# Holding the last two pairs' loads behind two divisions, and issuing the second k before the first weight quarter

## The chip, the cores and the metric

The kernel runs on one core of a Trainium2 chip. The metric is the device time of one execution in microseconds (us); the time given is the median over runs. Profiles come from one execution taken by the hardware profiler. TensorE (PE in the profile) multiplies matrices, VectorE (DVE) and ScalarE (ACT) work on tiles, GpSimd (POOL) issues the loads, SyncE (SP) issues the moves inside the chip and the stores.

## The reference

Two stages. First an attention in chunks: q, k and v have shape (8, 8, 576, 64) (batch, heads, positions, width), the 576 positions fall into 9 chunks of 64, and each chunk attends only to itself:

```python
scores = scale * np.matmul(q_c, k_c.transpose(0, 1, 2, 4, 3))
scores = scores - np.max(scores, axis=-1, keepdims=True)
attn = np.exp(scores)
attn = attn / (np.sum(attn, axis=-1, keepdims=True) + 1e-09)
out = np.matmul(attn, v_c)
```

The result, laid out as x of 4608 tokens by 512, goes through a feed-forward layer that multiplies two branches:

```python
a = x @ w1
b = x @ w2
h = a * b @ w3
return (h @ w_out).astype(np.float32)
```

w1 and w2 are 512 by 1024, w3 is 1024 by 1024, w_out is 1024 by 512. Inputs and output are float32.

## The kernel before

The 4608 tokens are cut into 18 *pairs* p of 256 tokens (four chunks of 64), numbered 0 to 17; two pairs make a *group* of 512 tokens. w3 @ w_out is worked out once on the chip (steps V, W, Z), so that the second half is (a * b) @ w3o.

The order of all work is written out by hand in the string `ORDER`. The kernel runs through it and calls one function for each step; each engine takes its instructions in that order (`tc.keep_in_program_order`), and an engine that waits holds back everything behind it. A step is a letter and its numbers:

- R, K: q and k of pair 0, loaded as float32 by SP and ACT and cast by ScalarE. q, k, v (lines of `load_qk`, `load_v`): loads of pair p, issued on POOL, with a cast to bfloat16 on the way. i0 to i3: a quarter of w1 and of w2, two loads each; o and h: w_out and w3. All of these go through POOL's one queue.
- T p.s (L188): VectorE transposes q (s = 0) or k (s = 1) of pair p. S: scores on TensorE. E (L221): exponential on ScalarE. P: weights times v, on TensorE. N p.u (L248, L251): reciprocal and division of half u of pair p, on VectorE, into `xn`. X (L263, L271): transpose of that half for the second stage.
- From pair 8 on, G (moves of the transposed q and k) and H (moves of the transposed x) are issued on SP, eight DMAs for each G or H of a group: four in G g.0 and four in G g.1.
- A p.j, B p.j: matmuls with w1 and w2; C (L317): ScalarE copies A's result out of PSUM; M (L332): VectorE multiplies it with B's. From pair 4 on one A, B, C, M serves a whole group of two pairs, so that they stand at even p only.
- O: matmuls with w3o; Y (L362): ScalarE copies the result; Q: SP stores it.
- D: dummy matmuls on a tile of zeros, into a PSUM buffer that the next step overwrites. D0 stands ahead of S1, D1 ahead of A0.0.

All results on TensorE go into one PSUM pool of four buffers of two banks. qk tiles have five buffers, `xn` three, v six fixed tiles (`vbuf[p % 6]`). All loads and matmuls go through the helpers `load` (L95) and `mm` (L92), so in the profile all matmuls have the line L92 and all of POOL's loads the line L95.

A load on POOL carries the semaphore that the eighth load before it counts up, and waits for it: eight loads are in flight at most.

Of the kernel before, what the change touches and what calls it, by code (L numbers as in the profile page):

```python
# [7 lines left out]

ORDER = """
R0 R1 v0 q1 i0 k1 v1 i1 i2 q2 k2 v2 i3 q3 k3 v3 q4 k4 v4 o h0 h1 D0.0.16.64 K0 T0.0 K1 T0.1 q5 k5 v5  # L10
S0 T1.0 E0 P0 D0.1.4.512 T1.1 q6 k6 v6 N0.0 S1 D1.0.5.512 X0.0 N0.1 X0.1 A0.0 E1 B0.0 C0.0 P1 M0.0
A0.1 N1.0 X1.0 B0.1 C0.1 N1.1 A0.2 X1.1 B0.2 C0.2 M0.1 A1.0 T2.0 B1.0 C1.0 M0.2 A1.1 T2.1 q7 k7 v7
B1.1 C1.1 M1.0 S2 M1.1 A0.3 E2 T3.0 B0.3 C0.3 P2 M0.3 A1.2 N2.0 X2.0 B1.2 C1.2 N2.1 A1.3 X2.1 B1.3
C1.3 M1.2 A2.0 T3.1 q8 k8 v8 B2.0 C2.0 M1.3 S3 T4.0 A2.1 E3 M2.0 B2.1 T4.1 q9 k9 C2.1 P3 v9 M2.1
A2.2 N3.0 B2.2 C2.2 X3.0 A2.3 N3.1 B2.3 X3.1 C2.3 M2.2 S4 M2.3 A3.0 E4 B3.0 C3.0 A3.1 M3.0 B3.1 C3.1
V0 A3.2 M3.1 B3.2 C3.2 V1 A3.3 M3.2 B3.3 C3.3 V2 W0 M3.3 V3 W1 Z0 V4 V5 W2 Z1 V6 V7 T5.0 Z2 W3 T5.1
q10 k10 T6.0 T6.1 P4 v10 q11 k11 Z3 S5 N4.0 O0 E5 X4.0 N4.1 X4.1 T7.0 O1 T7.1 Y0 Q0 T8.0 P5 v11 q12
k12 Y1 S6 T8.1 O2 Q1 E6 N5.0 X5.0 N5.1 X5.1 O3 T9.0 T9.1 Y2 G4.0 P6 v12 q13 k13 A4.0 N6.0 B4.0 G4.1
Y3 X6.0 N6.1 C4.0 A4.1 X6.1 B4.1 C4.1 M4.0 Q2 S7 Q3 M4.1 A4.2 E7 T10.0 B4.2 C4.2 T10.1 P7 v13 q14
k14 A4.3 M4.2 B4.3 N7.0 C4.3 A4.4 X7.0 M4.3 B4.4 C4.4 N7.1 A4.5 M4.4 B4.5 C4.5 X7.1 S8 M4.5 S9 E8  # L20
A4.6 T11.0 B4.6 E9 T11.1 P8 v14 q15 k15 C4.6 A4.7 M4.6 G5.0 B4.7 C4.7 N8.0 A6.0 M4.7 B6.0 N8.1 C6.0
G5.1 A6.1 X8.0 B6.1 M6.0 C6.1 X8.1 P9 v15 q16 k16 A6.2 M6.1 N9.0 B6.2 C6.2 N9.1 A6.3 M6.2 B6.3 C6.3
X9.0 A6.4 M6.3 B6.4 C6.4 X9.1 A6.5 T12.0 H4.0 B6.5 C6.5 M6.4 A6.6 M6.5 B6.6 T12.1 H4.1 C6.6 S10 S11
M6.6 E10 A6.7 T13.0 B6.7 E11 P10 v16 q17 k17 T13.1 C6.7 O4 M6.7 G6.0 N10.0 N10.1 X10.0 G6.1 P11 v17
Y4 X10.1 O5 N11.0 N11.1 Q4 X11.0 X11.1 T14.0 A8.0 H5.0 Y5 B8.0 T14.1 C8.0 A8.1 M8.0 B8.1 H5.1 C8.1
T15.0 A8.2 B8.2 M8.1 C8.2 T15.1 Q5 A8.3 B8.3 C8.3 M8.2 G7.0 S12 M8.3 S13 E12 A8.4 T16.0 B8.4 E13
G7.1 P12 T16.1 C8.4 A8.5 B8.5 M8.4 C8.5 N12.0 A8.6 M8.5 B8.6 C8.6 N12.1 A8.7 M8.6 B8.7 C8.7 X12.0
P13 M8.7 A10.0 X12.1 B10.0 C10.0 N13.0 A10.1 M10.0 B10.1 N13.1 C10.1 A10.2 X13.0 B10.2 M10.1 C10.2
X13.1 S14 S15 M10.2 E14 A10.3 H6.0 T17.0 B10.3 E15 P14 T17.1 C10.3 A10.4 H6.1 M10.3 B10.4 C10.4
N14.0 A10.5 M10.4 B10.5 G8.0 C10.5 N14.1 A10.6 M10.5 B10.6 C10.6 X14.0 P15 G8.1 X14.1 A10.7 M10.6  # L30
B10.7 N15.0 C10.7 O6 N15.1 M10.7 X15.0 X15.1 H7.0 S16 Y6 S17 O7 E16 E17 H7.1 P16 Y7 O8 Q6 N16.0 Q7
N16.1 X16.0 X16.1 P17 Y8 A12.0 N17.0 Q8 B12.0 N17.1 C12.0 A12.1 X17.0 B12.1 M12.0 C12.1 X17.1 A12.2
M12.1 H8.0 B12.2 C12.2 A12.3 M12.2 B12.3 C12.3 H8.1 A12.4 M12.3 B12.4 C12.4 A12.5 M12.4 B12.5 C12.5
A12.6 M12.5 B12.6 C12.6 A12.7 M12.6 B12.7 C12.7 O9 M12.7 O10 Y9 Q9 A14.0 Y10 B14.0 C14.0 Q10 A14.1
M14.0 B14.1 C14.1 A14.2 M14.1 B14.2 C14.2 A14.3 M14.2 B14.3 C14.3 A14.4 M14.3 B14.4 C14.4 A14.5
M14.4 B14.5 C14.5 A14.6 M14.5 B14.6 C14.6 A14.7 M14.6 B14.7 C14.7 O11 M14.7 O12 Y11 Q11 A16.0 Y12
B16.0 C16.0 Q12 A16.1 M16.0 B16.1 C16.1 A16.2 M16.1 B16.2 C16.2 A16.3 M16.2 B16.3 C16.3 A16.4 M16.3
B16.4 C16.4 A16.5 M16.4 B16.5 C16.5 A16.6 M16.5 B16.6 C16.6 A16.7 M16.6 B16.7 C16.7 O13 M16.7 O14
Y13 Q13 O15 Y14 Q14 O16 Y15 Q15 Y16 Q16 O17
"""  # L40


# [1 line left out]
def kernel(  # L44
# [11 lines left out]
    nc = tc.nc  # L56
    B, H, S, D = q.shape
# [18 lines left out]
    bf = mybir.dt.bfloat16  # L76
# [3 lines left out]
    consts = ctx.enter_context(tc.tile_pool(name="consts", bufs=1))  # L80
# [6 lines left out]
    def inorder(ins):  # L87
        tc.keep_in_program_order(ins)
        return ins

    def mm(*a, **kw):
        return inorder(nc.tensor.matmul(*a, **kw))  # L92

    def load(dst, src):
        return inorder(nc.gpsimd.dma_start(dst, src))  # L95

    def psum(name):
        return ps.tile([P, 2, 512], f32, tag="p", name=name)
# [7 lines left out]
    w3o = wpool.tile([P, FO, DM], bf, name="w3o")  # L106

    zero = consts.tile([P, 512], bf, name="zero")
    inorder(nc.vector.memset(zero[:], 0.0))
    vbuf = [consts.tile([P, 2, H, VW], bf, name=f"vbuf{i}") for i in range(6)]  # L110
    for t in vbuf:
# [2 lines left out]
    def spans(c0, n):  # L114

        at = 0
        while at < n:
            b, c = divmod(c0 + at, NCH)
            m = min(n - at, NCH - c)
            yield at, b, c, m  # L120
            at += m
# [19 lines left out]
    def heads(h):  # L141
        return slice(0, H) if h is None else slice(h * HH, (h + 1) * HH)

    def load_qk(p, which, h=None):
        if p not in qk_t:
            qk_t[p] = io.tile([P, 2, H, 2 * D], bf, tag="qk", bufs=5, name="qk")
        for s in which:
            for at, b, c, m in spans(4 * p, 4):
                load(qk_t[p][at * BL:(at + m) * BL, s, heads(h)],
                     (q, k)[s][b, heads(h), c * CH:(c + m) * CH, :].rearrange("h (p t) d -> p h (t d)", t=2))  # L150

    def load_v(p):
        for u in range(2):
            for at, b, c, m in spans(4 * p + 2 * u, 2):
                load(vbuf[p % 6][at * CH:(at + m) * CH, u, :, 0:D],
                     v[b, :, c * CH:(c + m) * CH, :].rearrange("h p d -> p h d"))
# [17 lines left out]
    qkT_t, qkm_t, s_t, e_t, pv_t, xn_t, xm_t, xt_t = {}, {}, {}, {}, {}, {}, {}, {}  # L174
# [106 lines left out]

    ab_t, ps_t, a_t, o_t = {}, {}, {}, {}

    def do_D(which, p, n, cols):

        d, key = (s_t, p) if which == 0 else (ps_t, (p, 0))
        if key not in d:
            d[key] = psum("z_ps")
        for _ in range(n):
            mm(d[key][:, 0, 0:cols], lhsT=zero[:, 0:P], rhs=zero[:, 0:cols], start=True, stop=True)  # L290
# [97 lines left out]
    def load_q(p, h=None):  # L388
        load_qk(p, (0,), h)

    def load_k(p, h=None):
        load_qk(p, (1,), h)
# [6 lines left out]
    def load_half3(i):  # L399
# [6 lines left out]

    do = {"q": load_q, "k": load_k, "v": load_v, "i": load_w12, "o": load_wo, "h": load_half3, "T": do_T, "S": do_S, "R": do_R, "K": do_K, "E": do_E, "G": do_G, "H": do_H,
          "P": do_P, "N": do_N, "X": do_X, "A": do_A, "B": do_B, "C": do_C, "M": do_M, "D": do_D, "V": do_V,  # L410
          "W": do_W, "Z": do_Z, "O": do_O, "Y": do_Y, "Q": do_Q}
    for step in ORDER.split():
# [31 lines left out]
```

The softmax here doesn't subtract the row's maximum and nothing guards it: scores larger than these inputs give would overflow.

## Time and profile before

| What | us |
|---|---|
| median of 5 runs | 245.42 (244.5 to 246.91) |
| the profiled execution | 245.42 |
| its span, first to last instruction | 243.3 |
| TensorE matmuls busy | 226.2 (93%) |
| VectorE busy | 153.8 (63%) |
| ScalarE busy | 85.1 (35%) |
| POOL busy (issuing loads) | 82.7 (34%) |

The span was run at a granted TensorE clock of 1.0. The median time from issue to landing of a load of 256 KB was 7.8 us for q, 10.6 us for k and 9.9 us for a weight piece; of SP's moves 6.4 us (qkm, 128 KB) and 3.3 us (xt, 64 KB); of a store of 512 KB 4.1 us. In a timeline a line reads: start, duration, engine, line, operation, output<-input, count; in brackets the idle time of the engine before it and what ended that.

### The profile page before, as it was taken

What the parts mean: (1) busy time and instruction counts of PE and PEld (TensorE: products, weight loads), DVE (VectorE), ACT (ScalarE), POOL (GpSimd) and SP (SyncE); (2) the same over time, 40 slices, a digit from 0 to 9 for tenths busy, and PEclk for the clock granted to TensorE, in tenths of its full rate; (3) what the DMA queues carried; (4) which work ended last, traced back from release to release, by engine and by line L of the source; (5) the groups of instructions that cost most, each with busy time, mean ns of one, the idle gap of its engine ahead of it and who ended that gap; (6) DMA issues with size and microseconds to landing.
All of it is one profiled execution on the core that took longest, in us unless ns stands there. A gap on an engine that the chain in (4) does not pass through costs nothing.

```text
span 243.3 us, 6344 instructions
## 1 busy us (share of the span) xinstructions
PE 226.2 (93%) x2731; PEld 120.5 (50%) x2753; DVE 153.8 (63%) x232; ACT 85.1 (35%) x116; POOL 82.7 (34%) x110
## 2 busy tenths in 40 slices
PE   1279989999999989999999999999999999999994
PEld 1238878874445444445444444444444444444443
DVE  1675899699799588999998899918440332143000
ACT  2411423423333344425336334162332432332322
POOL 8847876555985345763750000000000000000000
PEclk9999999999999999999999999999999999999999
DMA  7999999999999999999999923735502200400244
GB/s 178 181 183 180 185 168 201 196 194 169 162 173 218 224 225 260 176 220 194 205 217 255 287 62 80 172 86 202 149 0 89 86 0 0 172 3 1 86 172 172
DMA packets 93595, 37.63 MB, mean 155 GB/s; under 512 B 75008, under 2 KB 86528, under 8 KB 93568
## 3 DMA queue, kind: packets, MB, share of 16 engines
q0 software_dynamic: 82592, 18.88, 83.4%
q1 hardware_dynamic: 9936, 17.83, 24.2%
q10 hardware_dynamic: 1040, 0.52, 0.8%
q8 instruction: 21, 0.34, 0.6%
q14 instruction: 6, 0.05, 0.1%
HBM read 38.80 MB, written 9.44 MB: 198 GB/s over the span
## 4 chain that ended last, share of the span: by engine, by line
PE 77%; DMA 14%; DVE 2%; POOL 2%; issue 2%; ACT 1%; SPq 0%; ACTq 0%; DVEq 0%; POOLq 0%
PE ab_ps L92 43%; PE o_ps L92 24%; DMA w<-in_moe_w_dram 7%; PE w_ps L92 6%; DMA qk<-in_q_dram 3%; PE s_ps L92 3%; PE pv L92 2%; DMA qkm<-qkT 2%; DMA out_dram<-o_sb 2%; POOL vbuf L95 1%; ACT o_sb L362 1%; POOL w L95 1%; DVE xt L263 1%; DVE xn L251 1%; DVE qkT L188 1%
## 5 line engine op out<-in xcount | busy, mean ns | idle before, releaser
L92 PE MATMUL ab_ps<-xt,w 128*128 128x512 bf16 (+1 forms) x681 | 127.0, 342 | 1.7 <-DVE xt L263 1.1
L92 PEld LDWEIGHTS <-w 128*128 128x128 bf16 x704 | 67.2, 98 | 55.8 <-DVE xt L263 1.7
L332 DVE TENSOR_TENSOR ab<-a_sb,ab_ps 128x512 bf16<-128x512 f32 x71 | 47.8, 674 | 44.2 <-ACT a_sb L317 44.2
L317 ACT COPY a_sb<-ab_ps 128x512 f32<-128x512 f32 x71 | 41.6, 586 | 81.2 <-PE ab_ps L92 79.3
L92 PE MATMUL o_ps<-w3o,ab 128*128 128x512 bf16 (+1 forms) x285 | 63.3, 373 | 0.6
L188 DVE STREAM_TRANSPOSE qkT<-qk 128x1024 bf16<-128x1024 bf16 x36 | 45.0, 1289 | 9.6 <-ACT qk L139 5.5
L92 PEld LDWEIGHTS <-ab 128*128 128x128 bf16 x296 | 28.5, 98 | 32.3
L95 POOL DMA_DIRECT2D vbuf<-in_v_dram x40 | 33.9, 855 | 20.5 <-PE pv L92 4.3
L362 ACT COPY o_sb<-o_ps 128x1024 f32<-128x1024 f32 x17 | 17.2, 1012 | 45.5 <-PE o_ps L92 41.3
L251 DVE TENSOR_TENSOR xn<-pv,rc 128x512 bf16<-128x512 f32 x36 | 24.9, 692 | 1.2
L95 POOL DMA_DIRECT2D qk<-in_q_dram x23 | 18.1, 791 | 8.5 <-DMA vbuf<-in_v_dram 2.6
L95 POOL DMA_DIRECT2D qk<-in_k_dram x23 | 18.0, 787 | 7.1 <-DMA vbuf<-in_v_dram 4.3
L221 ACT ACTIVATE e<-s_ps 128x1024 bf16<-128x1024 f32 x16 | 15.9, 1027 | 1.9 <-PE s_ps L92 1.6
L92 PE MATMUL w_ps<-wo,w3T 128*128 128x512 bf16 x62 | 13.9, 379 | 0.1
L271 DVE STREAM_TRANSPOSE xm<-xn 128x512 bf16<-128x512 bf16 x20 | 13.6, 697 | 0.2
L248 DVE RECIPROCAL rc<-pv 128x8 f32<-128x8 f32 x36 | 6.9, 192 | 10.4 <-PE pv L92 10.4
L95 POOL DMA_DIRECT2D w<-in_moe_w_dram x16 | 11.1, 694 | 5.2 <-DMA wo<-in_moe_w_out_dram 2.9
L92 PEld LDWEIGHTS <-e 64*32 64x32 bf16 (+1 forms) x832 | 7.9, 97 | 7.9 <-issue 6.1
L263 DVE STREAM_TRANSPOSE xt<-xn 128x512 bf16<-128x512 bf16 x16 | 11.4, 712 | 0.5
L92 PE MATMUL pv<-vbuf,e 64*32 64x65 bf16 (+1 forms) x832 | 10.1, 198 | 1.1 <-ACT e L221 1.1
L92 PEld LDWEIGHTS <-qkT 32*64 32x64 bf16 x512 | 5.5, 117 | 11.0 <-DVE qkT L188 9.5
L355 DVE COPY o_sb<-o_ps 128x256 f32<-128x256 f32 x1 | 0.4, 426 | 16.0 <-PE o_ps L92 16.0
(23 smaller groups left out, 53.2 us busy)
## 6 DMA issues: line engine op xcount, KB each, us to landing
out_dram<-o_sb SPq DMA_DIRECT2D x17, 512.0 KB, 4.1
qkm<-qkT SPq DMA_DIRECT2D x40, 128.0 KB, 6.4
vbuf<-in_v_dram POOLq DMA_DIRECT2D x32, 128.0 KB, 8.7
w<-in_moe_w_dram POOLq DMA_DIRECT2D x16, 256.0 KB, 9.9
qk<-in_q_dram POOLq DMA_DIRECT2D x11, 256.0 KB, 7.8
qk<-in_k_dram POOLq DMA_DIRECT2D x11, 256.0 KB, 10.6
xt<-xm SPq DMA_DIRECT2D x40, 64.0 KB, 3.3
wo<-in_moe_w_out_dram POOLq DMA_DIRECT2D x4, 256.0 KB, 7.2
```

What stands on the lines that cost most here:

```text
L92: return inorder(nc.tensor.matmul(*a, **kw))
L95: return inorder(nc.gpsimd.dma_start(dst, src))
L188: inorder(nc.vector.transpose(qkT_t[g][:, :, p % 2, s, heads(h)].rearrange("p e h (y t) -> p h t e y", t=2), qk_t[p][:, s, heads(h)].rearr ...
L221: inorder(nc.scalar.activation(e_t[p][:, :, heads(hh)], s_t[p][:].rearrange("p u (h q) -> p u h q", q=CH)[:, :, heads(hh)], Exp, scale=sca ...
L248: inorder(nc.vector.reciprocal(rc[:], pv[:, :, :, D:W]))
L251: inorder(nc.vector.tensor_mul(xn_t[p][:, u], pv[:, :, :, 0:D], rc.to_broadcast([P, 2, 4, D])))
L263: inorder(nc.vector.transpose(new_xt(g)[:].rearrange("p (o t) -> p o t", o=KO)[:, :, t0:t0 + UT] .rearrange("p o (m y) -> p m o y", y=BL), ...
L271: inorder(nc.vector.transpose(xm_t[g][:, u, :, m].rearrange("p o (c y) -> p c o y", y=BL), xn_t[p][:].rearrange("p u r m d -> p (u r) m d" ...
L317: inorder(nc.scalar.copy(a_t[p, j][:], ps_t[p, j][:, 0, :]))
L332: inorder(nc.vector.tensor_mul(o, view(a_t.pop((p, j))[:]), view(ps_t.pop((p, j))[:, 1, :])))
L355: inorder(copy(o_sb[:, u, n0:n1], t[:, 0, 0:n1 - n0]))
L362: inorder(nc.scalar.copy(o_sb[:], ps_t.pop(p)[:]))
```

## The change

Two edits in `ORDER` and one new step, x. In the first line `i0 k1` becomes `k1 i0`: the load of k of pair 1 is issued ahead of the two loads of the first weight quarter. Further down, the loads of pair 16 (q, k from behind v15, v from behind P10) stand together behind N11.1 and a step x11; those of pair 17 stand together behind N12.1 and a step x12. A step x p copies one element of half 1 of `xn` of pair p into a tile of one element, on POOL, so that POOL waits until VectorE has divided that half; the loads that follow on POOL come after. POOL's order of loads is otherwise as it was: x11 comes directly behind v15, then q, k, v of pair 16, then x12, then q, k, v of pair 17, which end POOL's list.

The function w is added too, but no step calls it; D takes one more number, which names the same two tiles as before. On the other engines the instructions and their order stay as they are.

```diff
-R0 R1 v0 q1 i0 k1 v1 i1 i2 q2 k2 v2 i3 q3 k3 v3 q4 k4 v4 o h0 h1 D0.0.16.64 K0 T0.0 K1 T0.1 q5 k5 v5
+R0 R1 v0 q1 k1 i0 v1 i1 i2 q2 k2 v2 i3 q3 k3 v3 q4 k4 v4 o h0 h1 D0.0.0.16.64 K0 T0.0 K1 T0.1 q5 k5
...
-C6.0 G5.1 A6.1 X8.0 B6.1 M6.0 C6.1 X8.1 P9 v15 q16 k16 A6.2 M6.1 N9.0 B6.2
+C6.0 G5.1 A6.1 X8.0 B6.1 M6.0 C6.1 X8.1 P9 v15 A6.2 M6.1 N9.0 B6.2
...
-M6.6 E10 A6.7 T13.0 B6.7 E11 P10 v16 q17 k17 T13.1 C6.7 O4 M6.7 G6.0 N10.0 N10.1 X10.0 G6.1 P11 v17
-Y4 X10.1 O5 N11.0 N11.1 Q4 X11.0 X11.1
+M6.6 E10 A6.7 T13.0 B6.7 E11 P10 T13.1 C6.7 O4 M6.7 G6.0 N10.0 N10.1 X10.0 G6.1 P11 Y4 X10.1 O5
+N11.0 N11.1 x11 q16 k16 v16 Q4 X11.0 X11.1
...
-N12.1 A8.7 M8.6
+N12.1 x12 q17 k17 v17 A8.7 M8.6
...
+    tick = consts.tile([1, 1], bf, name="tick")
...
+    def do_x(p):
+
+        inorder(nc.gpsimd.tensor_copy(tick[:], xn_t[p][0:1, 1, 0, 0, 0:1]))
```

More of the change, by code (lines that the diff above doesn't have):

```diff
@@ L9 @@
 ORDER = """
-R0 R1 v0 q1 i0 k1 v1 i1 i2 q2 k2 v2 i3 q3 k3 v3 q4 k4 v4 o h0 h1 D0.0.16.64 K0 T0.0 K1 T0.1 q5 k5 v5
[L11 to L19, printed above, removed]
@@ L20 @@
-k14 A4.3 M4.2 B4.3 N7.0 C4.3 A4.4 X7.0 M4.3 B4.4 C4.4 N7.1 A4.5 M4.4 B4.5 C4.5 X7.1 S8 M4.5 S9 E8
-A4.6 T11.0 B4.6 E9 T11.1 P8 v14 q15 k15 C4.6 A4.7 M4.6 G5.0 B4.7 C4.7 N8.0 A6.0 M4.7 B6.0 N8.1 C6.0
-G5.1 A6.1 X8.0 B6.1 M6.0 C6.1 X8.1 P9 v15 q16 k16 A6.2 M6.1 N9.0 B6.2 C6.2 N9.1 A6.3 M6.2 B6.3 C6.3
-X9.0 A6.4 M6.3 B6.4 C6.4 X9.1 A6.5 T12.0 H4.0 B6.5 C6.5 M6.4 A6.6 M6.5 B6.6 T12.1 H4.1 C6.6 S10 S11
-M6.6 E10 A6.7 T13.0 B6.7 E11 P10 v16 q17 k17 T13.1 C6.7 O4 M6.7 G6.0 N10.0 N10.1 X10.0 G6.1 P11 v17
@@ L25 @@
[L25 to L36, printed above, removed]
@@ L37 @@
-B16.0 C16.0 Q12 A16.1 M16.0 B16.1 C16.1 A16.2 M16.1 B16.2 C16.2 A16.3 M16.2 B16.3 C16.3 A16.4 M16.3
-B16.4 C16.4 A16.5 M16.4 B16.5 C16.5 A16.6 M16.5 B16.6 C16.6 A16.7 M16.6 B16.7 C16.7 O13 M16.7 O14
-Y13 Q13 O15 Y14 Q14 O16 Y15 Q15 Y16 Q16 O17
+R0 R1 v0 q1 k1 i0 v1 i1 i2 q2 k2 v2 i3 q3 k3 v3 q4 k4 v4 o h0 h1 D0.0.0.16.64 K0 T0.0 K1 T0.1 q5 k5
+v5 S0 T1.0 E0 P0 D0.1.0.4.512 T1.1 q6 k6 v6 N0.0 S1 D1.0.0.5.512 X0.0 N0.1 X0.1 A0.0 E1 B0.0 C0.0 P1
+M0.0 A0.1 N1.0 X1.0 B0.1 C0.1 N1.1 A0.2 X1.1 B0.2 C0.2 M0.1 A1.0 T2.0 B1.0 C1.0 M0.2 A1.1 T2.1 q7 k7
@@ new lines @@
+v7 B1.1 C1.1 M1.0 S2 M1.1 A0.3 E2 T3.0 B0.3 C0.3 P2 M0.3 A1.2 N2.0 X2.0 B1.2 C1.2 N2.1 A1.3 X2.1
+B1.3 C1.3 M1.2 A2.0 T3.1 q8 k8 v8 B2.0 C2.0 M1.3 S3 T4.0 A2.1 E3 M2.0 B2.1 T4.1 q9 k9 C2.1 P3 v9
+M2.1 A2.2 N3.0 B2.2 C2.2 X3.0 A2.3 N3.1 B2.3 X3.1 C2.3 M2.2 S4 M2.3 A3.0 E4 B3.0 C3.0 A3.1 M3.0 B3.1
+C3.1 V0 A3.2 M3.1 B3.2 C3.2 V1 A3.3 M3.2 B3.3 C3.3 V2 W0 M3.3 V3 W1 Z0 V4 V5 W2 Z1 V6 V7 T5.0 Z2 W3
+T5.1 q10 k10 T6.0 T6.1 P4 v10 q11 k11 Z3 S5 N4.0 O0 E5 X4.0 N4.1 X4.1 T7.0 O1 T7.1 Y0 Q0 T8.0 P5 v11
@@ new lines @@
+q12 k12 Y1 S6 T8.1 O2 Q1 E6 N5.0 X5.0 N5.1 X5.1 O3 T9.0 T9.1 Y2 G4.0 P6 v12 q13 k13 A4.0 N6.0 B4.0
+G4.1 Y3 X6.0 N6.1 C4.0 A4.1 X6.1 B4.1 C4.1 M4.0 Q2 S7 Q3 M4.1 A4.2 E7 T10.0 B4.2 C4.2 T10.1 P7 v13
+q14 k14 A4.3 M4.2 B4.3 N7.0 C4.3 A4.4 X7.0 M4.3 B4.4 C4.4 N7.1 A4.5 M4.4 B4.5 C4.5 X7.1 S8 M4.5 S9
+E8 A4.6 T11.0 B4.6 E9 T11.1 P8 v14 q15 k15 C4.6 A4.7 M4.6 G5.0 B4.7 C4.7 N8.0 A6.0 M4.7 B6.0 N8.1
+C6.0 G5.1 A6.1 X8.0 B6.1 M6.0 C6.1 X8.1 P9 v15 A6.2 M6.1 N9.0 B6.2 C6.2 N9.1 A6.3 M6.2 B6.3 C6.3
+X9.0 A6.4 M6.3 B6.4 C6.4 X9.1 A6.5 T12.0 H4.0 B6.5 C6.5 M6.4 A6.6 M6.5 B6.6 T12.1 H4.1 C6.6 S10 S11
@@ new lines @@
+M6.6 E10 A6.7 T13.0 B6.7 E11 P10 T13.1 C6.7 O4 M6.7 G6.0 N10.0 N10.1 X10.0 G6.1 P11 Y4 X10.1 O5
+N11.0 N11.1 x11 q16 k16 v16 Q4 X11.0 X11.1 T14.0 A8.0 H5.0 Y5 B8.0 T14.1 C8.0 A8.1 M8.0 B8.1 H5.1
+C8.1 T15.0 A8.2 B8.2 M8.1 C8.2 T15.1 Q5 A8.3 B8.3 C8.3 M8.2 G7.0 S12 M8.3 S13 E12 A8.4 T16.0 B8.4
+E13 G7.1 P12 T16.1 C8.4 A8.5 B8.5 M8.4 C8.5 N12.0 A8.6 M8.5 B8.6 C8.6 N12.1 x12 q17 k17 v17 A8.7
+M8.6 B8.7 C8.7 X12.0 P13 M8.7 A10.0 X12.1 B10.0 C10.0 N13.0 A10.1 M10.0 B10.1 N13.1 C10.1 A10.2
+X13.0 B10.2 M10.1 C10.2 X13.1 S14 S15 M10.2 E14 A10.3 H6.0 T17.0 B10.3 E15 P14 T17.1 C10.3 A10.4
@@ new lines @@
+H6.1 M10.3 B10.4 C10.4 N14.0 A10.5 M10.4 B10.5 G8.0 C10.5 N14.1 A10.6 M10.5 B10.6 C10.6 X14.0 P15
+G8.1 X14.1 A10.7 M10.6 B10.7 N15.0 C10.7 O6 N15.1 M10.7 X15.0 X15.1 H7.0 S16 Y6 S17 O7 E16 E17 H7.1
+P16 Y7 O8 Q6 N16.0 Q7 N16.1 X16.0 X16.1 P17 Y8 A12.0 N17.0 Q8 B12.0 N17.1 C12.0 A12.1 X17.0 B12.1
+M12.0 C12.1 X17.1 A12.2 M12.1 H8.0 B12.2 C12.2 A12.3 M12.2 B12.3 C12.3 H8.1 A12.4 M12.3 B12.4 C12.4
+A12.5 M12.4 B12.5 C12.5 A12.6 M12.5 B12.6 C12.6 A12.7 M12.6 B12.7 C12.7 O9 M12.7 O10 Y9 Q9 A14.0 Y10
@@ L40 @@
+B14.0 C14.0 Q10 A14.1 M14.0 B14.1 C14.1 A14.2 M14.1 B14.2 C14.2 A14.3 M14.2 B14.3 C14.3 A14.4 M14.3
+B14.4 C14.4 A14.5 M14.4 B14.5 C14.5 A14.6 M14.5 B14.6 C14.6 A14.7 M14.6 B14.7 C14.7 O11 M14.7 O12
+Y11 Q11 A16.0 Y12 B16.0 C16.0 Q12 A16.1 M16.0 B16.1 C16.1 A16.2 M16.1 B16.2 C16.2 A16.3 M16.2 B16.3
+C16.3 A16.4 M16.3 B16.4 C16.4 A16.5 M16.4 B16.5 C16.5 A16.6 M16.5 B16.6 C16.6 A16.7 M16.6 B16.7
+C16.7 O13 M16.7 O14 Y13 Q13 O15 Y14 Q14 O16 Y15 Q15 Y16 Q16 O17
 """
@@ L150, in load_qk, with do_w @@
                      (q, k)[s][b, heads(h), c * CH:(c + m) * CH, :].rearrange("h (p t) d -> p h (t d)", t=2))
+    def do_w(p):
+        inorder(nc.gpsimd.tensor_copy(tick[:], qkT_t[p // 2][0:1, 0, p % 2, 1, 0, 0:1]))
+    def do_x(p):
+        inorder(nc.gpsimd.tensor_copy(tick[:], xn_t[p][0:1, 1, 0, 0, 0:1]))
     def load_v(p):
@@ L282, with do_D @@
     ab_t, ps_t, a_t, o_t = {}, {}, {}, {}
-    def do_D(which, p, n, cols):
-        d, key = (s_t, p) if which == 0 else (ps_t, (p, 0))
+    def do_D(which, p, j, n, cols):
+        d, key = ((s_t, p), (ps_t, (p, j)), (pv_t, (p, 0)))[which]
         if key not in d:
@@ L401, in load_half3 @@
         load_w3(i * n, (i + 1) * n)
-    do = {"q": load_q, "k": load_k, "v": load_v, "i": load_w12, "o": load_wo, "h": load_half3, "T": do_T, "S": do_S, "R": do_R, "K": do_K, "E": do_E, "G": do_G, "H": do_H,
+    do = {"q": load_q, "k": load_k, "v": load_v, "i": load_w12, "o": load_wo, "h": load_half3, "T": do_T, "S": do_S, "R": do_R, "K": do_K, "E": do_E, "w": do_w, "x": do_x, "G": do_G, "H": do_H,
           "P": do_P, "N": do_N, "X": do_X, "A": do_A, "B": do_B, "C": do_C, "M": do_M, "D": do_D, "V": do_V,
```

## The prediction

> **What bounds the kernel now.** I read the row of slices first, then the chain that ended last over the first 40 us, then the timelines of the two stretches that the diff touches. From the page (40 slices of 6.08 us, busy tenths):
>
> ```profile
> PE   1279989999999989999999999999999999999994
> ...
> PEclk9999999999999999999999999999999999999999
> DMA  7999999999999999999999923735502200400244
> ```
>
> Counted from 0, TensorE is full from slice 3 on, but for an 8 in slice 5 (30.4 to 36.5 us), one in the middle and the last. In the table of stretches it is idle for 8.5 us of the first 10, 2.4 us of the next 10, 1.1 us from 20 to 36, then 1.8 us in all until its last matmul ends at 240.04, with 3.3 us of tail. The DMA engines are full from slice 1 to 22 (140 us). So a change can gain in the first 36 us, or out of those 1.8 us, of which the biggest piece (0.56 us at 87.3) is put down to no engine or DMA. It can lose anywhere after 36 us.
>
> What ends the start-up, in the chain (start, us, what):
>
> ```profile
> 23.48 7.23 DMA qk<-in_q_dram
> ...
> 30.74 1.33 DVE qkT L188
> ...
> 35.83 1.92 PE ab_ps L92 x16
> ```
>
> q of pair 3 lands at 30.71 (issued 23.48). VectorE's queue is in order: the transpose T3.0 waits for that landing, and behind it stand M0.3 and the divisions and transposes of pair 2 (N2, X2), which A2.0 on TensorE waits for until 35.83. TensorE itself never waits longer than 0.56 us after that: 35.83 + about 204 us = 240.04.
>
> **Part 1: the second k ahead of the first weight quarter.** The timeline of the start:
>
> ```profile
> 3.98 1.48 POOL L95 DMA_DIRECT2D w<-in_moe_w_dram  x2
> 5.45 0.89 POOL L95 DMA_DIRECT2D qk<-in_k_dram  x1
> ...
> 13.69 1.30 DVE L188 STREAM_TRANSPOSE qkT<-qk 128x1024 bf16<-128x1024 bf16 x1 [2.81 <-DMA qk<-in_k_dram]
> ...
> 15.04 1.07 PE L92 MATMUL z_ps<-qkT 32*64 32x64 bf16 x64 [0.73 <-DVE qkT L188]
> ```
>
> Three load issues swap: k1 leaves at 3.98 instead of 5.45, the two weight pieces at 4.87 and 5.6 instead of 3.98 and 4.7. No instruction is added. q1, ahead in the queue, lands at 3.11 + 6.4 = 9.5. Next come w1 at 3.98 + 6.9 = 10.9, w2 at about 12.2 and k1 at 5.45 + 8.2 = 13.65, so a k costs some 1.5 to 1.8 us of the queue: k1 should land near 11.2, the weights near 12.5 and 13.7. T1.1 then ends near 12.5 instead of 14.99. S1 cannot follow all the way: ahead of it on TensorE stand the four dummy matmuls of D0 (from about 12.4, each start 0.43 us after the last: end near 14.1). S1 goes from 15.04 to about 14.1, then 1.0 us of S1 and five dummies of 0.43 us, and A0.0 starts near 17.25 instead of 18.15. The weights are in by then, and X0.1 is done near 15.9. So TensorE's first real work comes 0.9 us earlier.
>
> The Trainium skill speaks against even that: "TensorE: Matmul & The Clock Gate" (Part 1: The HAM clock gate) says that TensorE runs at half its clock until some 3.4 us of sustained work are seen, in a window that doesn't move with the kernel. The row: the dummies start 0.43 us apart up to 18.15, and the 16 matmuls of A0.0 and B0.0 from 18.15 to 19.8 start 0.11 us apart, so in this execution the clock rose about when the dummies ended; the PEclk digits of 9 do not show it. If the window stays in place, an A0.0 moved to 17.25 runs cold until about 18.1: its first four matmuls of 256 columns take 0.21 instead of 0.11 us each, and of the 0.9 us about 0.45 is left. By the row alone the gain is 0.9 us, by the rule about half.
>
> Neither reaches the end. q3, the 22nd load of its queue, has the same loads ahead of it in another order, and the DMA engines are busy all the while (188 GB/s from 16 to 23 us, 178 from 23 to 31). POOL holds at most eight loads in flight: the 11th issue waits for the 3rd, and so on. After the swap the 12th waits for k1 (11.2) instead of w1 (10.9), the 13th for w1 (12.5 instead of w2's 12.2), from the 15th on nothing differs. That is 0.3 us later for two issues, with seven transfers in flight, so the engines don't run dry. I put q3's landing at 30.7, T3.0 at 30.74 and A2.0 at 35.83 as before: TensorE comes to A2.0 earlier and waits 1.2 to 1.7 us instead of 0.77. **Cost of part 1: 0.0 us.** From both sides: q3 0.4 us later (two delayed issues, handed on in full) costs 0.4. A gain cannot exceed the idle time before A2.0, 0.77 + 0.9 = 1.7 us, and needs q3 in by 29.0.
>
> **Part 2: the hold.** It adds two copies of one element on POOL (x11 after N11.1, x12 after N12.1) and moves six of POOL's loads behind them. Such a copy is not in the trace; the nearest rows are POOL's one-column memsets of 0.1 us, and 0.1 to 0.3 us counts for nothing, since POOL has no other work left. What queues behind them is all of POOL's rest: q, k, v of pairs 16 and 17, at the very end of its list. The rows (POOL's loads, VectorE, TensorE's weight load):
>
> ```profile
> 116.83 0.88 POOL L95 DMA_DIRECT2D qk<-in_q_dram  x1
> 118.21 0.88 POOL L95 DMA_DIRECT2D qk<-in_k_dram  x1 [0.49 <-DMA qk<-in_q_dram]
> ...
> 132.26 2.49 DVE L188 STREAM_TRANSPOSE qkT<-qk 128x1024 bf16<-128x1024 bf16 x2
> ...
> 137.00 0.69 DVE L251 TENSOR_TENSOR xn<-pv,rc 128x512 bf16<-128x512 f32 x1
> ...
> 139.41 4.88 PEld L92 LDWEIGHTS <-w 128*128 128x128 bf16 x24 [0.18 <-DMA qkm<-qkT]
> ...
> 146.04 2.50 DVE L188 STREAM_TRANSPOSE qkT<-qk 128x1024 bf16<-128x1024 bf16 x2
> ```
>
> Pair 11's second division starts at 121.50 and ends at 122.2, pair 12's (137.00) at 137.7. So q16 is issued at 122.3 instead of 116.83 and k16 at 123.2; q17 at 137.9 instead of 121.37, k17 at 138.8, v17 until 141.4. They are due when T16.0, T16.1, T17.0 and T17.1 start: 132.26, 133.5, 146.04 and 147.3. The v's are due only at P16 and P17 (162.7 and 166.6).
>
> How long a load takes is the unknown. The nearest rows for pair 17 are q and k issued at 59.93 and 60.81 after a pause of the queue: 4.7 and 5.3 us. That gives 142.6 and 144.1, 3 us ahead of need. The worst rows, a full queue at 70.33 and 71.34, are 12.3 and 12.8 us; but in the trace the DMA engines run empty near 140, and no load is ahead of q17 any more, so I take the short end. For pair 16: v15 has landed at 122.1, so its queue is empty too, but SP's moves (H5 from 124.39) and the 512 KB store at 122.81 share the engines. Rows: 4.7 and 5.3 empty, 7.8 and 11.9 as pair 16 ran before. I take about 7: 130, against 133.5.
>
> If that cover is gone, TensorE pays at once. PSUM has four buffers, which I take to be handed round in turn. A8.6 needs the one that M8.4 frees at 135.31 behind T16.1, and starts at about 135.34; A10.5 needs the one that M10.3 frees at 149.08 behind T17.1, and starts at about 149.29. So a late k16 costs its whole delay, a late pair 17 its delay less 0.2 us.
>
> What the hold can give: the DMA engines carry less between 116 and 138, when H5 (124.39 to 133.04) and G7 (133.77 to 140.2) are moved on SP. Their landings, 7.0 to 5.3 us for H5 and 5.5 for G7's first moves, fall to 2.0 to 2.4 us after 144 when no load is under way. Who waits for them: A10.0, 0.18 us at 139.41; S14 at 144.71 does not. G7 should be through before q17 starts, so the load brought to 138 hits only its last moves. **Part 2: -0.2 us**; the bounds are 0 and, if both loads lag as in the worst rows, +4 us.
>
> **Sum:** 0.0 - 0.2. The span goes from 243.3 to 243.1. The profiled execution took 245.42 us, 2.1 us around its span; that is also the median of the five runs (244.5 to 246.91). So **245.2 us**.
>
> **Rivals.** *Start-up gain reaches the end (18%).* If k1 and the scores of pair 1 out of the way let q3 land earlier, or H5 holds TensorE longer in most executions than in this one, 0.7 to 1.9 us come off: 243.5 to 244.7. For it: the chain's start is load-bound; against it: the same bytes lie ahead of q3, and A10.0's wait is 0.18.
> *The held loads arrive late (25%), slower.* The place is T17.0 or T16.1 in VectorE's queue. It decides when q17 takes over 8.1 us, k17 over 8.7, or k16 over 10.3. With 12.3 and 12.8 us k17 lands at 151.6, T17.1 ends at 152.9 instead of 148.54 and TensorE loses 4.2 us: 249.6. With k16 at 11.9 us it lands at 135.1, 1.6 us late: 247.0. For it: 20 us of cover are cut to 3; against it: the DMA engines are empty when pair 17 is issued.
> *The hold holds nothing* is out: POOL is done with v15 at 116.7 and the divisions end at 122.2 and 137.7.
>
> **How the numbers follow.** My forecast has 57%; with the spread of runs it lies within 244.4 to 246.2. The range goes from 244.1 (part of the first rival) to 247.1 (pair 16 late by 1.6, or pair 17 by 2). About 0.5%, 1.2 us, is what a measurement of this kernel tells from no change. Faster: 0.03 from the forecast and 0.13 of the first rival, 0.16. Slower: 0.03 and 0.20 of the late loads, 0.23. The rest, 0.61, is the same.
>
> **What would show it.** Right: T1.1 near 11.3 and A0.0 near 17.3, but T3.0 still at 30.7 and A2.0 near 35.8 with a longer wait before it; q16 at 122.3, q17 at 137.9, T17.0 still near 146 without a wait for a DMA; no wait at A10.0. Wrong: A2.0 well before 35.3; a DMA wait at T16 or T17, and TensorE idle near 135 or 149.

## The result, and the profile after

The changed kernel takes 245.01 us (median of 43 runs, 243.84 to 246.79); the kernel before, on the same chips, 245.60 (80 runs). The ratio is 0.9974, with a 95% interval of 0.9962 to 0.9985: 0.26% faster, within the half per cent that the prediction called the same, and inside its range. The profiled execution took 244.69 us with a span of 242.9. Of the executions timed further down, three ran in a slower state of the chip (two of the kernel before, one of the run that holds only pair 17) and are left out of every mean and count.

The page's slices of the changed kernel:

```profile
PE   1289979999999989999999999999999999999994
...
PEclk9999999999999999999999999999999999999999
DMA  7999999999999999999999893736502200400244
```

TensorE is as full as before. The DMA row shows the hold: slice 22 (134 to 140 us) falls from 9 to 8, slice 23, in which pair 17 now arrives, rises from 2 to 9. The chain over the start:

```profile
23.36 7.39 DMA qk<-in_q_dram
...
30.78 1.33 DVE qkT L197
...
35.87 1.92 PE ab_ps L92 x16
```

q3 lands at 30.75 (before: 30.71) and A2.0 starts at 35.87 (35.83): in this pair of profiles the start gains nothing, as foretold. The timeline of the start (all engines, then TensorE's own):

```profile
3.97 0.91 POOL L95 DMA_DIRECT2D qk<-in_k_dram  x1
4.83 1.48 POOL L95 DMA_DIRECT2D w<-in_moe_w_dram  x2
...
6.97 5.33 DVE L197 STREAM_TRANSPOSE qkT<-qk 128x1024 bf16<-128x1024 bf16 x4 [5.42 <-ACT qk L140]
...
14.19 1.06 PE L92 MATMUL z_ps<-qkT 32*64 32x64 bf16 x64
...
17.07 0.82 PE L92 MATMUL z_ps<-xt,w 128*128 128x256 bf16 x6
...
18.25 1.25 PE L92 MATMUL z_ps<-xt,w 128*128 128x256 bf16 x10 [0.36 <-issue]
```

k1 is in by 10.95, so that the four transposes run through; S1 starts at 14.19 instead of 15.04 and A0.0 at 17.07 instead of 18.15. Its seventh matmul waits until 18.25 for nothing that the timeline names. P1, which follows, comes at 19.43 instead of 20.05: 0.6 us of the 0.9 are left. VectorE then stands still for 1.72 us ahead of T3.0 instead of 1.05.

This wait caps what an earlier A0.0 can bring. Seven profiles, this one among them, have the swap. In five of them the seventh matmul of A0.0 starts at 18.25 or 18.26, even where A0.0 began at 16.31, and in a sixth at 18.79. In all six a transfer of 16 KB on the DMA queue for instructions begins 2.3 to 2.5 us before that. The wait may be one for TensorE's next instructions; no run moved that transfer, so this is not shown.

The stretch of the hold (POOL, VectorE, TensorE's weight load):

```profile
122.49 0.18 POOL L159 COPY tick<-xn 1x1 bf16<-1x1 bf16 x1 [3.58 <-DVE xn L260]
122.73 0.88 POOL L95 DMA_DIRECT2D qk<-in_q_dram  x1
...
132.13 2.50 DVE L197 STREAM_TRANSPOSE qkT<-qk 128x1024 bf16<-128x1024 bf16 x2
...
137.70 0.18 POOL L159 COPY tick<-xn 1x1 bf16<-1x1 bf16 x1 [11.46 <-DVE xn L260]
138.54 0.88 POOL L95 DMA_DIRECT2D qk<-in_q_dram  x1 [0.66 <-issue]
...
139.28 4.88 PEld L92 LDWEIGHTS <-w 128*128 128x128 bf16 x24 [0.17 <-issue]
145.91 2.48 DVE L197 STREAM_TRANSPOSE qkT<-qk 128x1024 bf16<-128x1024 bf16 x2
```

q16 took 6.0 us and k16 8.7, q17 4.6 and k17 5.2. Neither T16 nor T17 waits here: k16 is 1.1 us early, q17 2.8 and k17 2.5. But A10.0 waits as before, 0.17 us, and not for a DMA: the 0.18 us that the prediction put down to a move was no such wait.

The 0.4 us between these two spans lies in no step of the change. TensorE's last work ends 0.41 us earlier, and the stretch from 167 to 181 us, where no load runs in either kernel, is 0.3 of that. A gain of 0.26% over dozens of executions can't be read from one profile of each. So the experiments were timed over many executions, and each left a profile.

### The profile page after: what moved, and what is told of

It reads as the page before. It is cut to its first block, busy times and chain, and to the rows that moved or that the text cites. A ratio compares the mean times of both kernels' runs of the same rounds, so it can differ in the third digit from the quotient of the medians.

```text
span 242.9 us, 6347 instructions
## 1 busy us (share of the span) xinstructions
PE 225.7 (93%) x2731; PEld 120.2 (49%) x2753; DVE 153.8 (63%) x232; ACT 85.0 (35%) x116; POOL 83.1 (34%) x112
## 4 chain that ended last, share of the span: by engine, by line
PE 81%; DMA 10%; DVE 3%; POOL 2%; issue 2%; ACT 0%; DVEq 0%; POOLq 0%
PE ab_ps L92 45%; PE o_ps L92 26%; PE w_ps L92 6%; DMA w<-in_moe_w_dram 4%; DMA qk<-in_q_dram 3%; DMA qk<-in_k_dram 3%; PE s_ps L92 3%; PE pv L92 3%; DVE xn L260 1%; POOL vbuf L95 1%; POOL w L95 1%; DVE xt L272 1%; DVE qkT L197 1%; DVE xm L280 1%; DVE ab L341 0%
```

## The experiments

The ratios are against the kernel before on the same chip. Beside them stands the span of the timed executions of all chips together, mean and standard error, and how many were above 244.3 us:

| Kernel | Ratio (95% interval) | Executions | Mean span, us | Above 244.3 |
|---|---|---|---|---|
| before, all | 1 | 200 | 243.71 ± 0.06 | 46 |
| swap only | 0.9979 (0.9957 to 1.0001) | 22 | 243.43 ± 0.17 | 4 |
| hold only, two runs | 0.9993 (0.9969 to 1.0017), 0.9981 (0.9965 to 0.9998) | 36 | 243.39 ± 0.10 | 1 |
| both, with the repeat | 0.9974 (0.9962 to 0.9985), 0.9971 (0.9953 to 0.9988) | 66 | 243.12 ± 0.06 | 1 |
| six dummies, two runs | 0.9993 (0.9966 to 1.0020), 0.9992 (0.9964 to 1.0019) | 28 | 243.41 ± 0.14 | 4 |
| hold and six dummies | 0.9971 (0.9952 to 0.9989) | 22 | 242.93 ± 0.10 | 0 |
| both, pair 17 right behind 16 | 0.9973 (0.9953 to 0.9992) | 22 | 243.21 ± 0.12 | 2 |
| swap, only pair 17 held | 0.9989 (0.9970 to 1.0007) | 21 | 243.41 ± 0.15 | 2 |

### One half at a time

```diff
-R0 R1 v0 q1 i0 k1 v1        (swap only; the rest as before)
+R0 R1 v0 q1 k1 i0 v1
```

> Only the second k ahead of the first weight quarter, loads of pairs 16 and 17 as before. Theory of the prediction (the start's gain ends at the landing of q3, 30.7 us): A0.0 at about 17.1 us, A2.0 at 35.8, time against the kernel before 0.0% (within 0.1%). Rival (the start carries the measured 0.26%): 0.25% faster, with A2.0 at about 35.2 in most executions.

The hold only is the changed kernel with `i0 k1` put back:

> Only the hold, start as before. If the hold carries the measured 0.26%: 0.25% faster than the kernel before, A0.0 at 18.15 us and A2.0 at 35.8. If it gives nothing, as the two profiles suggest (A10.0 starts 0.53 us after P13 with and without it): within 0.1%.

And both together once more:

> The changed kernel once more on the same chip as the two halves. If the 0.26% is real: 0.15 to 0.4% faster than the kernel before, and the sum of the two halves. If the two halves sum to zero, so does this.

The mean span falls by 0.28 ± 0.18 us with the swap, by 0.32 ± 0.11 with the hold (two runs), and by 0.59 ± 0.08 with both: the halves add up. The swap alone is not clear of nothing; on top of the hold it gives 0.27 ± 0.11. The first run of the hold alone gave a ratio of 0.9993 and looked like nothing; only with the second run (below) is it clear. The two act differently. The hold takes away the upper tail: almost a quarter of the executions of the kernel before lie above 244.3, one in 36 with the hold alone. The swap alone keeps 4 of 22 there, but lowers the median span from 243.6 to 243.1.

The profile of the repeat shows what the hold can cost (VectorE, TensorE):

```profile
133.06 1.32 DVE L197 STREAM_TRANSPOSE qkT<-qk 128x1024 bf16<-128x1024 bf16 x1 [0.23 <-DMA qk<-in_k_dram]
...
134.98 3.61 PE L92 MATMUL ab_ps<-xt,w 128*128 128x512 bf16 x16 [0.20 <-DVE ab L341]
```

Here k16, issued at 123.02, took 10.0 us. T16.1 waits 0.23 us for it, and A8.6 on TensorE hands 0.20 us of that on. So the cover of 1.1 us in the first profile of the changed kernel can be used up; this is the prediction's second rival, on a small scale.

Why the start matters is in the profile of the hold alone, whose start is that of the kernel before (TensorE, VectorE, TensorE):

```profile
18.30 3.12 PE L92 MATMUL z_ps<-xt,w 128*128 128x256 bf16 x16
...
30.90 1.31 DVE L197 STREAM_TRANSPOSE qkT<-qk 128x1024 bf16<-128x1024 bf16 x1
...
36.68 1.81 PE L92 MATMUL ab_ps<-xt,w 128*128 128x256 bf16 x15 [0.32 <-DVE xt L272]
```

In the profile before, the same matmuls read:

```profile
18.15 1.96 PE L92 MATMUL z_ps<-xt,w 128*128 128x256 bf16 x16
```

With only the hold the first twelve of the 16 matmuls of A0.0 and B0.0 start 0.21 us apart, the rest 0.11, as all but the first do in the profile before: TensorE ran at half its clock until about 20.8 us. By T3.0 the delay is larger than the wait for q3. T3.0 waits for no DMA, and A2.0 starts at 36.68, 0.85 us later than before. So the landing of q3 does not set A2.0 in an execution in which the clock rises this late.

### Filling the idle gap instead

Ahead of S1 TensorE stood idle from 14.1 to 15.0 in the kernel before, in the middle of its first busy stretch. The swap removes this gap; so do two more dummy matmuls, which move no load and leave S1 and A0.0 where they are:

```diff
-D0.1.4.512
+D0.1.6.512
```

> The kernel before, with six dummy matmuls instead of four ahead of S1, so that TensorE does not stand idle from 14.1 to 15.0 us; S1 and A0.0 stay where they were (15.0 and 18.15 us), no load moves. Theory (the idle gap ahead of S1 puts off the rise of TensorE's clock, and the swap removes the gap): the clock is up before A0.0 in the profile (dummies or A0.0 0.21 and 0.11 us apart), and the kernel is about 0.2% faster than before, as with the swap. Rival (the swap gains because A0.0 starts 0.9 us earlier, whatever the clock): 0.0%.

It ran a second time, since the first run could not tell:

> The kernel before with six dummy matmuls instead of four ahead of S1, once more: alone it gave 0.07% (interval from 0.34% faster to 0.20% slower), with the hold 0.46 us of mean span against the hold alone. Theory (the gap ahead of S1 costs time through TensorE's clock): mean span 0.3 to 0.4 us under the kernel before on the same chip, ratio 0.9985. Rival (the gap costs nothing, the run with the hold was luck): the same mean, ratio 1.000. Both: no load is held, so a fifth of the executions stays above 244.3 us.

And on top of the hold:

> Only the hold (k behind the first weight quarter as before), with six dummy matmuls instead of four ahead of S1. Theory (the swap gains through TensorE's clock, which the idle gap ahead of S1 holds down in some executions): the profile shows the clock up before A0.0, and the mean span is 243.15, as with both parts. Rival (the earlier start itself gains): 243.5, as with the hold alone.

The kernel before ran again for a second profile, and the hold alone for its mean:

> The kernel before once more, for a second profile of its start. Theory: the clock rises at a time that differs from one execution to the next, at 18.2 us or later (A0.0 either 0.11 or 0.21 us a matmul), and A2.0 lies between 35.8 and 36.7 us. Time 0.0% against itself, within 0.15%.

> Only the hold once more, on the same chip as the run with six dummies, for its mean span and a second profile. Both theories: mean span 243.5 (0.12% faster than the kernel before), no execution above 244.5, G6's last move landing before 129 us.

The kernel before gave 1.0001 (0.9979 to 1.0022) against itself; in mean span its 14 executions lie 0.30 ± 0.21 us below the 43 others of that chip, and that difference is noise. TensorE in the run with the hold and six dummies:

```profile
15.00 0.91 PE L92 MATMUL z_ps<-qkT 32*64 32x64 bf16 x64
15.84 1.25 PE L92 MATMUL z_ps<-zero 128*128 128x512 bf16 x4
...
18.06 1.91 PE L92 MATMUL z_ps<-xt,w 128*128 128x256 bf16 x16 [0.97 <-DVE xt L272]
```

The dummies behind S1 are done in 1.25 us: the clock is up by 15.84, 2.2 us before A0.0. Over all profiles, by the spacing of the matmuls: with neither swap nor more dummies (four of them) the clock rises about when the dummies end, at 18.2 to 18.4, in three, and in one at 20.8. With the gap filled (three) the dummies behind S1 speed up by about 17.1 at the latest. With the swap, A0.0 itself, 0.9 us earlier, is nowhere all at half clock (in one profile its first three matmuls are slow). Counted from S1 at 15.0 to 15.2 us, the clock rises about 3 to 6 us later in the four profiles with the gap; counted from P0 at 11.6 to 12.0, about 3 to 6 us later in the ten without it. So the gap acts as if the count began anew behind it; no run varied its length.

Filling the gap gives 0.29 ± 0.15 us alone and 0.46 ± 0.14 on top of the hold, as much as the swap (0.28 and 0.27), although A0.0 is not earlier. Alone it is not shown: each run has an interval that holds 1, and against the kernel before on their own chips the two runs give 0.06 ± 0.23 and 0.46 ± 0.27. On top of the hold it is clearer, 0.39 ± 0.16 against the hold alone on the same chip. That the earlier start itself gains is not borne out, and not excluded. The hold with the six dummies has the lowest mean of all, 242.93, but is not clear of the changed kernel's 243.12 (0.19 ± 0.12 us below it; the ratios are 0.9971 and 0.9974).

How the gain reaches the end stays open in part. In the twelve profiles in which T3.0 has its old place and the clock is up in time, A2.0 starts 5.1 us after q3 lands, whatever stands ahead of it; there a gain at the start can reach A2.0 only through q3. The cold start, 0.85 us in one profile of four, makes some 0.2 us. Besides, q3 landed at 30.6 us on average in the ten profiles with the swap or the dummies, and at 30.8 in the four without; no run tells whether that is chance. The two together are of the size measured, but so few profiles fix neither.

### Moving the transposes that wait for q3

```diff
-A0.3 E2 T3.0 B0.3 C0.3 P2 M0.3 A1.2 N2.0 X2.0 B1.2 C1.2 N2.1 A1.3 X2.1 B1.3 C1.3 M1.2 A2.0 T3.1
+A0.3 E2 B0.3 C0.3 P2 M0.3 A1.2 N2.0 X2.0 B1.2 C1.2 N2.1 A1.3 X2.1 T3.0 T3.1 B1.3 C1.3 M1.2 A2.0
```

> The changed kernel with the transposes T3.0 and T3.1 put behind X2.1 on VectorE. Theory (q3's landing at 30.7 us holds A2.0 only because T3.0 stands ahead of N2 and X2 in VectorE's queue): A2.0 at about 34.9 instead of 35.8 us; S3 then waits for T3.1 until about 37.2, which gives 0.4 us back; 0.2% faster than the changed kernel, 0.45% faster than the kernel before. Rival (something else holds A2.0, such as PSUM or TensorE itself): A2.0 stays at 35.8, no gain.

The ratio against the kernel before is 0.9974 (0.9957 to 0.9991), the same as without this edit. TensorE in its profile:

```profile
31.37 5.41 PE L92 MATMUL ab_ps<-xt,w 128*128 128x256 bf16 x48
...
37.15 0.71 PE L92 MATMUL s_ps<-qkT 32*64 32x64 bf16 x64 [0.36 <-DVE qkT L197]
...
45.00 2.25 PE L92 MATMUL ab_ps<-xt,w 128*128 128x256 bf16 x19 [0.38 <-DVE xt L272]
```

A2.0 now follows A1.3 without a break, near 35.0. So T3.0 in VectorE's queue was what held it, as the chain said. But S3 waits 0.36 us for T3.1, and the matmuls at 45.0 wait 0.38 us for the next transpose (without the edit they start at 45.20 and follow at once). Most of what A2.0 gained is handed back within 10 us, because VectorE has the same work to do before it.

### Which load, and whom it delays

The first run with six dummies and no hold caught the stall that the hold removes (TensorE; below it the same step in the profile before, and in the second run with six dummies):

```profile
130.23 0.21 PE L92 MATMUL s_ps<-qkm 64*64 64x64 bf16 x1
131.13 1.01 PE L92 MATMUL s_ps<-qkm 64*64 64x64 bf16 x63 [0.69 <-DMA xt<-xm]
```

```profile
130.76 0.71 PE L92 MATMUL s_ps<-qkm 64*64 64x64 bf16 x64
```

```profile
130.18 1.11 PE L92 MATMUL s_ps<-qkm 64*64 64x64 bf16 x64
```

This is S12. It needs the eight moves of G6, issued on SP from 116.9 us on. In the first of these profiles the last one, issued at 121.8, took 9.2 us and landed at 131.0, and S12 took 1.2 us longer than in the profile before. (The profile names a move of x as what ended the wait. That move shares a semaphore with G6's last one; no move of x landed before 132.9.) In the second run S12 took 0.4 us longer; the landing of its last move is missing from the trace. In the six profiles with pair 16 not held the last moves of G6 took 7.4 to 9.2 us; in the eight with pair 16 behind x11 they took 2.3 to 5.6, and S12 lost nothing. The two stalls make 0.27 us over the six profiles, near the 0.32 ± 0.11 of the hold. In the profile before the last move took 7.6 us and landed at 129.4, with S12 at 130.76: 1.3 us of cover. One pair of loads was held at a time, with the swap in both:

```diff
-N11.1 x11 q16 k16 v16 Q4 ... N12.1 x12 q17 k17 v17
+N11.1 x11 q16 k16 v16 q17 k17 v17 Q4 ... N12.1
```

> The changed kernel with pair 16 held behind x11 and pair 17 issued right behind it, without x12. Theory (the loads issued between 117 and 122 us slow G6's eight moves, which S12 needs at 130.5; x11 alone frees those 5 us): the last move of G6 lands in under 6 us, before 129, as in the changed kernel; span mean 243.2, almost no execution above 244.3. Rival (what matters is pair 17 out of the way of H5 and G7 after 126 us): mean 243.4 and a fifth of the executions above 244.3, as with the swap alone.

The other holds only pair 17; q16 and k16 stand behind v15, v16 behind P10 again:

> The changed kernel with pair 16 loaded as before and only pair 17 held behind x12. Theory: pair 16's loads still run beside G6, so that its last move takes 7 us or more and lands within 1 us of S12 in the profile; mean span about 243.4, with executions above 244.3 as with the swap alone. Rival (pair 17 is what matters): as the changed kernel, mean 243.2, none above 244.3.

With pair 16 held the last move of G6 took 3.6 us and the mean span is 243.21, not clear of the changed kernel's 243.12. With only pair 17 held it took 7.4 us and the mean is 243.41, as with the swap alone. So G6 goes with pair 16, as foretold; in time the two runs differ by 0.20 ± 0.19 us, which is not clear of nothing. Both profiles show another trouble (TensorE; first with only pair 17 held, then with pair 16 held and 17 right behind it):

```profile
145.76 0.93 PE L92 MATMUL s_ps<-qkm 64*64 64x64 bf16 x63 [1.61 <-DMA qkm<-qkT]
```

```profile
144.41 1.04 PE L92 MATMUL s_ps<-qkm 64*64 64x64 bf16 x64
```

That is S14, which needs the moves of G7. With only pair 17 held these are issued from 133.2 to 139.1, and pair 17's q and k leave at 137.6 and 138.5, beside the last of them: the last move took 6.5 us. With pair 17 right behind pair 16 its loads run beside all of G7: the last move took 6.4 us and landed at 144.38, and S14, at 144.41, took 1.04 us instead of 0.71. In the changed kernel, with both pairs held, the last move took 2.4 us, and S14 lost nothing. So holding pair 16 frees G6, and it takes both holds to free G7; what x12 adds in time is too small for these runs (0.10 ± 0.14 us).

The same trouble stands earlier, at S10, which needs G5's moves: in five of the fourteen profiles, with the hold and without it, the last of these landed just as S10 began or up to 0.4 us later, and S10 took 0.4 to 0.7 us longer than without a wait. No edit here touches it.

### Too late a load

```diff
-N12.1 x12 q17 k17 v17 A8.7 ... N13.1 C10.1
+N12.1 A8.7 ... N13.1 x13 q17 k17 v17 C10.1
```

> The changed kernel with pair 17 held until pair 13 is divided (143.4 us instead of 137.6). Theory of the prediction (four PSUM buffers in turn, A10.5 stands behind T17.1 and M10.3): q17 issued at 144.2, lands at 148.9 (4.6 us), k17 at 150.3, T17.1 ends at 151.6 instead of 148.4, TensorE idle 3.0 us before A10.5: 3.0 us (1.2%) slower than the changed kernel. Rival (VectorE's slack before 163 us takes the delay up): less than 1 us slower.

The ratio is 1.0221 (1.018 to 1.0263); the median is 250.92 us, 5.9 above the changed kernel. The profiled execution, 252.26 us, is the slowest of the six. POOL, VectorE, TensorE and its weight loads:

```profile
144.67 0.88 POOL L95 DMA_DIRECT2D qk<-in_q_dram  x1 [0.66 <-issue]
...
151.50 2.73 DVE L197 STREAM_TRANSPOSE qkT<-qk 128x1024 bf16<-128x1024 bf16 x2 [5.20 <-DMA qk<-in_q_dram]
...
154.84 5.55 PE L92 MATMUL ab_ps<-xt,w 128*128 128x512 bf16 x16 [5.19 <-DVE ab L341]
...
156.92 0.15 PEld L92 LDWEIGHTS <-w 128*128 128x128 bf16 x1 [0.27 <-issue]
```

VectorE waits 5.20 us at T17.0 and TensorE 5.19 us at A10.5, for M10.3: the delay goes to TensorE whole, which fits four PSUM buffers that go round in turn. q17 took 6.8 us, not 4.6, beside H6's moves on SP from 144.47. And after the idle time nine matmuls of 512 columns start 0.43 us apart instead of 0.22: 1.9 us more, which the expectation left out. The page's row of the granted clock has it too, in slices 24 and 25 (150 to 163 us; 0.50 from 155 to 157):

```profile
PEclk9999999999999999999999996899999999999999
```

## Why the prediction was right or wrong

The range held, and so did "the same"; the forecast of 0.1% was too small, and the 0.26% comes from two places that it had named for nothing or not at all. That the time still lay in the range is in part luck: the 0.2 us of the forecast was put at a wait that stayed as it was.

*"Cost of part 1: 0.0 us."* The steps of the timeline were right within 0.3 us: k1 in by 10.95 (11.2 foretold), S1 14.19 (14.1), A0.0 17.07 (17.25), q3 30.75 (30.7), A2.0 35.87 (35.83). The conclusion failed, at the step from one profiled start to all: the term put at nothing measured 0.28 ± 0.18 us with the swap alone and 0.27 ± 0.11 on top of the hold. In the profiled start the clock rose at 18.15, as the prediction itself had seen; it asked what the clock would do to the changed kernel, and not what it does to the kernel before in another execution. The rule of the Trainium skill ("TensorE: Matmul & The Clock Gate", Part 1: The HAM clock gate), that the clock rises only after some 3.4 us of sustained work, was brought in against the change. The profiles agree with it, with a rise about 3 to 6 us after work without the gap begins. In the runs it is the likelier reason for the gain, since the gap ahead of S1 sits in the stretch that has to count as sustained.

*"Who waits for them: A10.0, 0.18 us at 139.41."* The mechanism, lighter DMA engines for SP's moves, was right; the place was not. A10.0 still waits 0.17 us with the hold. The moves that matter are G6's, issued just where pair 16's loads ran; the prediction went through H5 and G7 and left G6 out, though its last landing had 1.3 us of cover. In place of 0.2 us always, S12 stalls in a share of the executions (1.2 and 0.4 us in two profiles of six); on average the hold is worth 0.32 ± 0.11 us. The rows that it read for the moves were partial, too: H5's took 8.5 to 5.3 us, G7's 6.2 down to 2.5, and those after 144 us 1.9 to 3.7.

*The late loads.* Pair 17's landing times were right (4.7 and 5.3 us foretold, 4.6 and 5.2 measured), and so was the place where a late load costs and that it costs its delay; the price lacked the clock. Pair 16 took 6.0 and 8.7 us instead of about 7, and T16 didn't wait; in the repeat k16 took 10.0 us, and T16.1 waited 0.23 us, which the prediction had named as a sign of being wrong.

*"Start-up gain reaches the end"*, the first rival, came true in part, through executions in which TensorE, not q3, is late; whether q3 also lands earlier is open. Its 0.7 us or more was too large.

## What to carry to other kernels

When one profile shows a step hidden behind a wait by less than a microsecond, the other executions can lie on the other side; ask for each such wait how far what stands behind it varies, and time many executions before calling an edit worth nothing. To find what a transfer disturbs, list every transfer issued in the same stretch with the time it is needed, and look at the one with the least cover, not at the wait that the trace happens to show. A load held back spends its cover and may meet the next transfer: after a hold, go through the list again, for what it now meets and for how late it lands itself.

## What the runs showed that was not expected

- An idle time of 5.2 us put TensorE back to half its clock for 3.8 us (nine matmuls at 0.43 us), as the spacing of the matmuls and the row of the granted clock show. The cold start shows in the spacing alone: there the row has 9s in every kernel.
- Two dummy matmuls of 0.43 us, filled into an idle gap at the start, were worth 0.46 ± 0.14 us of the mean span on top of the hold; alone, 0.29 ± 0.15, they are not clear of nothing.
- A move of 128 KB inside the chip took 2.3 us with no load of q or k under way (the last moves of G7 in the run with the late load) and up to 9.2 us with such loads.
- After its copy of one element POOL took another 0.06 to 0.66 us before the next load's issue began.
